# Softmax attention mixed with feature-map attention on one core: VectorE gets more key tiles in the first three query blocks, and the first score slots are computed in halves

## The chip, the cores and the metric

The kernel runs on one core of a Trainium2 chip. The metric is device time in microseconds (us) of one execution. Five engines work side by side, each through its own list in order: TensorE (PE in the profile, its weight loads PEld), ScalarE (ACT), VectorE (DVE), GpSimd (POOL) and SyncE (SP), which here issues most DMAs.

## The reference, cut to what matters

Two attentions of 32 heads with 16 channels each read the same x (2048 rows of 512). A replaces the exponential by a small learned feature map and is linear in the length; B is plain softmax attention. A gate of x mixes the two.

```python
q, k, v = (x @ wqkv) in heads                       # for A and for B, each with its own wqkv, wo
# A: phi = softmax(+-(q @ w_phi)); o = phi_q @ (phi_k^T v) / (phi_q @ sum(phi_k))
# B:
scores = einsum("bhqd,bhkd->bhqk", q, k) * Dh**-0.5
p = softmax(scores)
o = einsum("bhqk,bhkd->bhqd", p, v)
out = g * (o_A @ wo_A) + (1 - g) * (o_B @ wo_B)     # g = sigmoid(x . gate_w)
```

The bulk is B: 32 heads times 2048 by 2048 exponentials.

## The kernel before, in words

**Blocks, tiles, slots.** B is cut into 32 blocks. A block is a chunk of 512 queries for four heads (i = 0 to 3). For each of its heads there are 16 key tiles (kt = 0 to 15) of 128 keys, so a block has 64 score tiles of 128 keys by 512 queries. Blocks 0 and 1 use the same keys (row 0 of kT_B) and the same queries, with the two parities of qz.

**Two engines make exponentials.** Most tiles go to ScalarE, two tiles of one PSUM pair at a time: a *slot*. TensorE writes the two score tiles side by side (qk_mm, L990), ScalarE takes the exponential of 1024 columns in one instruction (add_exp, L1080) into one of the 12 slots of the buffer E (ERING, L76). The other tiles go to VectorE: it turns a score tile into int16 that, read as bf16, is a rough exponential (L1066; two tiles joined in one instruction of 1024 columns, L1056, where TABLE's "pairs" says so). Four such tiles are a group; GpSimd adds a constant to a group's words twice (shifted, L1042), and the three versions are each multiplied with V, so that a tile of VectorE costs three products with V and a tile of ScalarE one. DN (L31) says how many tiles of each block VectorE takes. Before, the VectorE tiles of a block are the last key tiles of each head (L912); next_tile gives ScalarE the others, counted up from 0 (L918).

**Closing a block.** All products with V of a block (L1101) add up in one PSUM bank, psO. When the last is done, VectorE copies psO to Tf (L1196), and only then can the products of the next block begin. Until then ScalarE can run ahead by the 12 slots of E.

**Start.** The first 512 rows of x come by two DMAs (L673, one issued by SP, one by ACT), are turned by TensorE against an identity (X0 to X3, L1494) and copied out (Xe0 to Xe3, L1500 on ACT for Xe1, L1503 on DVE for the others). The other three chunks of x come by DMA transposes, issued by SP one after the other (L678: x1_0 to x1_3, x2_0 to x2_3, x3_0 to x3_3). Keys and queries of chunk 0 come first: Q0.00 and Q0.01 are the two 256-column halves of the query product (L867, copied out by L874 on ACT and L876 on DVE), K0.00 makes key tile 0 (L824, copied out by L830 on ACT), K0.01 the key tiles 1 to 3 (copied out by L832 on DVE). K0.1, K0.2, K0.3 make the keys of the chunks 1 to 3 (L750 for the products, L817 for the copies). Before all that TensorE runs eight products of constants (warm, L701).

**Order.** Nothing is decided at run time. TABLE (L81) holds for each engine the full order of its operations as numbers, the place of each in the order of creation; place() walks these lists, and -1 in TensorE's list stands for an idle filler, four products with a zero weight (zero_mm, L1091). Before there are 14 fillers, all in the first blocks. Numbers of SP before: 0 is the first x DMA, 15 and 16 are weights for queries and values of the first heads, 2 to 13 are the DMA transposes x1_0 to x3_3, 17 to 19 the rest of the B weights, 20 to 27 DMA transposes of A's weights (wat).

Of the kernel before, what the change touches and what calls it, by code (L numbers as in the profile page):

```python
# [590 lines left out]
def _build(ctx, nc, A_x, A_wqkv, A_w_phi, A_wo, B_wqkv, B_wo, gate_w, out):  # L591
# [106 lines left out]
    def warm_fn(e):  # L698
        ins = None
        for _ in range(8):  # L700
            ins = e.matmul(psM, lhsT=ones[:, 0:128], rhs=ones, start=True, stop=True)  # L701
        return ins
# [927 lines left out]
```

## Time and profile before

| | us |
|---|---|
| median of 3 runs (662.16 to 662.63) | 662.53 |
| the profiled execution, own time | 662.22 |
| its span, first to last instruction | 660.4 |
| ACT busy in the span | 639.3 |
| DVE busy in the span | 603.7 |
| POOL busy in the span | 403.9 |

PE's busy time (651.3 us) is that of matmuls whose ends are modelled and overlap, so it is not to be read as the load of the array. The time of 662.22 us lies 1.8 us above the span: work around the first and the last instruction that the trace does not show.

### The profile page before, as it was taken

The page shows a single profiled execution, that of the slowest core. Times are in us where ns is not written, and L with a number is a line of the kernel's source. Part 1 is how long each engine was busy: PE and PEld are TensorE (multiplying, and loading weights), DVE is VectorE, ACT ScalarE, POOL GpSimd, SP SyncE. Part 2 cuts the span into 40 slices and gives each one's busy share as a digit, 9 for nine tenths or more (in the row PEclk, how much of TensorE's full clock was granted, in tenths as well). Part 3 has the DMA queues.
Part 4 walks back from the last instruction along what each step waited for, and adds up shares of the span by engine and source line. Part 5 has one row for each costly group of instructions (what it writes and reads, how often), then busy time and mean ns, then how long its engine had stood idle before and what let it go on. Part 6 is the DMA issues. An engine that isn't in the chain of part 4 may idle for free.

```text
span 660.4 us, 20511 instructions
## 1 busy us (share of the span) xinstructions
PE 651.3 (99%) x8752; PEld 228.4 (35%) x8752; DVE 603.7 (91%) x971; ACT 639.3 (97%) x723; POOL 403.9 (61%) x431
## 2 busy tenths in 40 slices
PE   9999999999999999999999999999999999999997
PEld 4332333434333333433333233322333233332333
DVE  4699889999998898999999999999999989999985
ACT  6999999999999999999999999999989999999996
POOL 7058457565665437575566776576766657665853
PEclk9999999999999999999999999999999999999999
DMA  6530101001010000000113221123201333024231
GB/s 136 106 91 11 34 7 28 11 7 31 6 28 11 12 18 10 16 20 11 25 40 92 78 41 53 47 65 76 59 26 60 94 82 72 18 67 108 58 80 36
DMA packets 67915, 30.94 MB, mean 47 GB/s; under 512 B 53176, under 2 KB 62776, under 8 KB 67824
## 3 DMA queue, kind: packets, MB, share of 16 engines
q1 hardware_dynamic: 66352, 28.95, 18.6%
q8 instruction: 69, 1.13, 0.7%
q10 hardware_dynamic: 1088, 0.66, 0.3%
q0 software_dynamic: 384, 0.02, 0.1%
q14 instruction: 22, 0.18, 0.1%
HBM read 7.87 MB, written 8.88 MB: 25 GB/s over the span
## 4 chain that ended last, share of the span: by engine, by line
PE 70%; ACT 22%; DVE 8%; issue 1%; POOL 0%; POOLq 0%
PE psO L1101 26%; PE psS L990 24%; ACT E_t L1080 20%; PE psS L750 13%; DVE Tx_t L1066 2%; PE psS L1382 2%; PE psS L841 1%; DVE oT_t L1066 1%; ACT EA_t L1375 1%; DVE Tz_t L1066 1%; DVE Ty_t L1066 1%; PE psS L1479 1%; PE psS L854 1%; ACT phiK_t L1375 1%; PE psS L701 1%
## 5 line engine op out<-in xcount | busy, mean ns | idle before, releaser
L1080 ACT ACTIVATE E_t<-psS 128x1024 bf16<-128x1024 f32 x652 | 610.6, 1095 | 9.5 <-PE psS L990 8.6
L990 PE MATMUL psS<-qz_t,kTB_t 32*128 32x512 bf16 x2048 | 271.0, 384 | 3.8 <-ACT E_t L1080 1.8
L1066 DVE TENSOR_SCALAR Tx_t<-psS 128x512 int16<-128x512 f32 x252 | 166.3, 681 | 8.8 <-PE psS L990 7.7
L990 PEld LDWEIGHTS psS<-qz_t,kTB_t 32*128 32x128 bf16 x2048 | 73.8, 91 | 229.3 <-ACT E_t L1080 109.4
L1101 PE MATMUL psO<-E_t,vaug_t 128*32 128x512 bf16 x1304 | 124.0, 385 | 0.5 <-DVE Tf_t L1196 0.3
L1066 DVE TENSOR_SCALAR Ty_t<-psS 128x512 int16<-128x512 f32 x122 | 81.1, 682 | 5.8 <-PE psS L990 4.8
L1042 POOL INT64_ADD vA_t<-vA_t x72 | 71.4, 995 | 15.1 <-PE psO L1101 13.7
L1042 POOL INT64_ADD Ty_t<-Ty_t x42 | 43.5, 1037 | 19.3 <-PE psO L1101 19.3
L1042 POOL INT64_ADD Ty_t<-Tx_t x29 | 30.0, 1036 | 37.1 <-DVE Tx_t L1066 33.0
L1101 PE MATMUL psO<-vA_t,vaug_t 128*32 128x512 bf16 (+1 forms) x520 | 50.5, 384 | 0.1
L1101 PEld LDWEIGHTS psO<-E_t,vaug_t 128*32 128x32 bf16 x1304 | 31.4, 95 | 43.8 <-issue 31.9
L1066 DVE TENSOR_SCALAR Tz_t<-psS 128x512 int16<-128x512 f32 x64 | 43.0, 683 | 1.9 <-PE psS L990 1.5
L1101 PE MATMUL psO<-Ty_t,vaug_t 128*32 128x512 bf16 (+1 forms) x436 | 44.2, 384 | 0.0
L1066 DVE TENSOR_SCALAR oT_t<-psS 128x512 int16<-128x512 f32 x60 | 40.3, 681 | 2.1 <-PE psS L990 1.7
L1042 POOL INT64_ADD vA_t<-Tx_t x22 | 22.6, 1029 | 29.4 <-DVE Tx_t L1066 21.5
L1066 DVE TENSOR_SCALAR WAT_t<-psS 128x512 int16<-128x512 f32 x58 | 38.9, 681 | 0.9 <-PE psS L990 0.5
L1066 DVE TENSOR_SCALAR vA_t<-psS 128x512 int16<-128x512 f32 x58 | 38.6, 682 | 0.7 <-PE psS L990 0.6
L1066 DVE TENSOR_SCALAR Wp_t<-psS 128x512 int16<-128x512 f32 x54 | 36.5, 683 | 1.4 <-PE psS L990 0.8
L1042 POOL INT64_ADD WoA_t<-Tz_t x18 | 19.5, 1082 | 27.5 <-DVE Tz_t L1066 27.4
L750 PE MATMUL psS<-xT_t,WB_t 128*32 128x512 bf16 x480 | 36.0, 383 | 0.1
L750 PE MATMUL psS<-Wp_t,xT_t 128*32 128x512 bf16 x512 | 35.8, 382 | 0.0
L1042 POOL INT64_ADD oT_t<-Ty_t x18 | 17.8, 991 | 20.4 <-DVE Ty_t L1066 19.0
(162 smaller groups left out, 873.2 us busy)
## 6 DMA issues: line engine op xcount, KB each, us to landing
dpq<-EA_t SPq DMA_DIRECT2D x16, 256.0 KB, 2.1
Rb_t<-lr SPq DMA_DIRECT2D x120, 32.0 KB, 1.9
dpo<-kv_t SPq DMA_DIRECT2D x16, 128.0 KB, 1.8
qz_t<-qz_t SPq DMA_DIRECT2D x120, 16.0 KB, 1.8
Tf_t<-Tf_t SPq DMA_DIRECT2D x60, 32.0 KB, 2.0
WB_t<-in_B_wqkv_dram SPq DMA_DIRECT2D x3, 384.0 KB, 3.7
out_dram<-WvA_t SPq DMA_DIRECT2D x8, 128.0 KB, 2.0
out_dram<-WB_t SPq DMA_DIRECT2D x6, 128.0 KB, 1.9
```

The source lines that it names most:

```text
L701: ins = e.matmul(psM, lhsT=ones[:, 0:128], rhs=ones, start=True, stop=True)
L750: ins = e.matmul(out[32 * i:32 * i + 32, :], lhsT=lhsT[:, 32 * i:32 * i + 32], rhs=rhs, start=start, stop=stop, tile_position=(0, 32 * i))
L841: mms = [lambda e, ap, i=i, t=t: e.matmul(ap[:, 128 * i:128 * (i + 1)], lhsT=xT[:, t, NQ * c + 128 * i:NQ * c + 128 * (i + 1)], rhs=W_B[:, ...
L854: mms = [lambda e, ap, i=i, t=t: e.matmul(ap[:, 256 * i:256 * (i + 1)], lhsT=xT[:, t, NQ * c + 128 * (2 * hf + i):NQ * c + 128 * (2 * hf + ...
L990: return e.matmul(bank, lhsT=kT_B[32 * i:32 * i + 32, ROW[b // 2] % 2, 128 * kt:128 * (kt + 1)], rhs=qz[32 * i:32 * i + 32, b // 2 % 4, b ...
L1042: op = P.add("pool", P64 + W64 * size, d_prio(g["ts"][0]) - 5.0 + (0.0 if key == "s" else M_LATE), lambda e: e.int64_add(words(dst), words ...
L1066: ops.append(drain(f, mm, "dve", 0.70, d_prio(d), lambda e, ap, q=q: e.tensor_scalar(quarter(tb, q).bitcast(I16), ap, EXPB, 0.0, op0=ALU.a ...
L1080: op = P.add("act", EXP_OVH + 0.4267 * n, 0.0, lambda e: e.activation(Ebuf[:, j // 2 % EPAIRS, 512 * SZ[0] * (j % 2):512 * SZ[0] * (j % 2) ...
L1101: return e.matmul(psO[32 * i:32 * i + w, :], lhsT=vaug[:, kt, o:o + w], rhs=rhs, start=start, stop=stop, tile_position=(0, 32 * i), skip_g ...
L1375: ins = e.activation(dst.rearrange("p (g s c) -> p s g c", s=2, c=64)[:, sgn, :, :], ap.rearrange("p (g c) -> p g c", c=64), ACTF.Exp, sca ...
L1382: mms = [lambda e, ap, n=n, f=f: e.matmul(ap[:, 64 * n:64 * n + 64].rearrange("p (s g j) -> p s g j", s=2, j=4), lhsT=ident[:], rhs=es[n][ ...
L1479: mms = [lambda e, ap, g=g: e.matmul(ap[:, 64 * g:64 * g + 64], lhsT=qT(g)[:, 128 * j:128 * (j + 1)], rhs=kzbd[:, g, 0:64], start=True, st ...
```

## The change

DN's first three entries go from 6, 20, 20 to 16, 24, 18: 58 instead of 46 VectorE tiles, and so 646 instead of 652 ScalarE slots. SOON names the key tiles that VectorE takes in the blocks 0 and 1: in block 0 the last of each x chunk (3, 7, 11, 15) for all four heads, in block 1 also 14 and 13. ScalarE gets the others in rising order. HALVES = 3: the first three slots are computed in two halves of 256 queries; the three first halves need only the first half of the queries. The first x chunk comes by four DMAs of 128 rows, each with its own landing; the value weights of the first heads move from SP to ACT. The key product of the first chunk is in three pieces (key tile 0, key tile 1, key tiles 2 and 3). The warm-up has six products, and the waits that tied V0.0 and the second query half to other work are gone.

```diff
-DN = (6, 20, 20, 24, 26, 26, 26, 20, 22, 22, 24, 18, 26, 24, 20, 26, 30, 22, 24, 26, 22, 24, 30, 26, 18, 22, 36, 18, 24, 24, 32, 16)
+DN = (16, 24, 18, 24, 26, 26, 26, 20, 22, 22, 24, 18, 26, 24, 20, 26, 30, 22, 24, 26, 22, 24, 30, 26, 18, 22, 36, 18, 24, 24, 32, 16)
...
+HALVES = 3
+SOON = ((3, 7, 11, 15), (3, 7, 11, 15, 14, 13))
...
-    for i in range(2):
-        dma(("sp", "act")[i], -0.01, lambda e, i=i: e.dma_start(
-            xs[:, 2 * i:2 * i + 2, :], A_x[0, 256 * i:256 * (i + 1), :].rearrange("(i p) c -> p i c", p=128)), [("xs", 2 * i), ("xs", 2 * i + 1)],
+    for i in range(4):
+        dma(("sp", "act")[i % 2], -0.01, lambda e, i=i: e.dma_start(xs[:, i, :], A_x[0, 128 * i:128 * (i + 1), :]), [("xs", i)],
...
-        for _ in range(8):
+        for _ in range(6):
...
-        for n, (lo, hi) in enumerate(((0, 128), (128, NQ))):
+        for n, (lo, hi) in enumerate(((0, 128), (128, 256), (256, NQ))):
...
-            if n == 0:
-                for op in q_half[1]:
-                    op.deps = op.deps + [ke]
...
-        for op in q_half[1]:
-            op.deps = op.deps + q_half[0]
...
-            dtiles.append(dict(t=(b, i, NT - dcount[b][i]), k=k))
+            dtiles.append(dict(t=(b, i, SOON[b][k // 4] if b < len(SOON) else NT - dcount[b][i]), k=k))
...
-                    t = (cur, i, done[cur][i])
+                    t = (cur, i, own[cur][i][done[cur][i]])
...
+        if j < HALVES:
+            for n in range(2):
+                def part(e, n=n):
+                    for m, t in enumerate(ts):
+                        ins = qk_mm(e, t, psS[:, 512 * (f.bank.index + m) + 256 * n:512 * (f.bank.index + m) + 256 * (n + 1)], n)
+                    return ins
...
+        if j < HALVES:
+            ops = []
+            for h in range(2):
+                def part(e, h=h):
+                    cols = slice(256 * h, 256 * (h + 1))
...
-    second = add_qk(1)
-    for op in P.ops:
-        if op.name == "V0.0.0":
-            op.deps = op.deps + [second]
+    add_qk(1)
```

TABLE is replaced as a whole: all five orders, "pairs" (38 joined VectorE instructions before, 56 after) and the PSUM banks. TensorE's list has 2 fillers instead of 14, GpSimd's 433 entries instead of 427, and VectorE's 966 instead of 971. In VectorE's list 62, 87 and 116 instructions stand ahead of the copies that close the blocks 0, 1 and 2 (59, 82 and 111 before); 6, 9 and 11 of them are joined ones (1, 1 and 3 before). The first line of SP's order:

```diff
-        0, 15, 16, 2, 3, 4, 5, 6, 7, 9, 8, 13, 10, 12, 11, 25, 23, 27, 24, 21, 17, 26, 20, 22, 128, 19, 18, 28, 129, 942, 943, 1066, 1068,
+        0, 17, 2, 4, 5, 6, 7, 9, 10, 11, 8, 12, 28, 15, 21, 13, 19, 14, 25, 24, 26, 22, 30, 29, 23, 132, 27, 133, 967, 968, 20, 1094,
```

In the new numbers 0 and 2 are the x DMAs of rows 0 to 127 and 256 to 383, 17 the first query weights, 4 to 15 the transposes x1_0 to x3_3, 28 a transpose of A's weights, 21 and 19 the rest of the value and query weights (384 KB each). So the last piece of the third chunk, 14 (x3_2), stands behind 28, 21 and 19. ACT issues 1 (x rows 128 to 255), 16 (key weights), 3 (x rows 384 to 511) and 18 (value weights), and then runs Xe1, the copy of K0.00, the copy of the first query half, and the halves of the slots 1, 2, 0, first halves first. TensorE's list begins warm, X0, X1, K0.00, Q0.00, K0.01, X2, X3, the first halves of the slots 1, 2 and 0, Q0.01, K0.02, their second halves, V0.0.

More of the change, by code (lines that the diff above doesn't have):

```diff
@@ L357 @@
-        "25040123"
+        "6706724520747524307462074350234503254104261046230540135230526350263502356105431043620541304205360462105410346013546026104264052301"
+        "2513052035065420642560520632560235102241054250613056452056240624506205462450264045260452405265402065246024502640532650642056236052"
+        "4504620523605642053265042604526406524062406524065260245560425650246054265042502654062554026054260542654306520456204254062540562403"
+        "0642560452065240526045625064265032065246024650420562305246024560235065240642360235602460254052410651360253065230645205320654256024"
@@ new lines @@
+        "6052605206520465424063260244502604241061254065204562406250462503260546206240562405264506205462504625406256034206524065246025064526"
+        "0624506426054260545260243061542146026045204526405625042654062540526045426045265024650426025604652402654062045625046256024605246054"
+        "2605624025054526052306246052452042560420534256406254016532054362045246504250624052356025604256032506325042045260456245026045624056"
+        "2045620524654065240562356023650245042560425063460253620320253230562540624602546054205426056240625406520356324305425065246052605320"
@@ new lines @@
+        "4354103461063510643013015042065240652460452064526045240625605260256045204520625046524650245604256406524065204526540620563250304640"
+        "5620542654206526024506425064250624603256024506254062540526406425046240563205632053602360230642650246506325032506245604265024502406"
+        "5236024546204650624604526402425406310360234504520635461502145054264062504625045216450620452640526045625406240625640254064250632502"
+        "4065230562406532045304526044205246054260426052450265406254026504256054260542062460542065240625406256045265042052545026506325062405"
@@ L358 @@
+        "642054205046206"
     ),
@@ L808, in _build @@
     kv_mm, va_free, wp_ops = [], [], []
-    kkey = lambda r, kt: ("kT", 0, "a") if r == 0 and kt < 1 else ("kT", r % 2, kt // 4)
+    kkey = lambda r, kt: ("kT", 0, "ab"[kt]) if r == 0 and kt < 2 else ("kT", r % 2, kt // 4)
     xk = lambda c: [("xT", t, c) for t in range(KT)]
@@ L817, in k_fill @@
         drain(f, mm, eng, 0.69, prio, lambda e, ap: e.tensor_copy(kT_B[:, r % 2, NQ * c:NQ * (c + 1)], ap),
-              writes=[("kT", r % 2, c)] + [("kT", 0, "a")] * (r == 2 and c == 0), name=f"Ke{r}.{c}")
+              writes=[("kT", r % 2, c)] + [("kT", 0, "a"), ("kT", 0, "b")] * (r == 2 and c == 0), name=f"Ke{r}.{c}")
     q_half = [[], []]
     def k_first(prio):
-        for n, (lo, hi) in enumerate(((0, 128), (128, NQ))):
-            f, mm = fill(prio + 0.15 * n - 0.015 * (n == 0), [lambda e, ap, t=t, lo=lo, hi=hi: e.matmul(
+        for n, (lo, hi) in enumerate(((0, 128), (128, 256), (256, NQ))):
+            f, mm = fill(prio + 0.15 * n, [lambda e, ap, t=t, lo=lo, hi=hi: e.matmul(
                 ap[:, lo:hi], lhsT=W_B[:, t, D:D + 128], rhs=xT[:, t, lo:hi], start=(t == 0), stop=(t == KT - 1))
-                for t in range(KT)], ["wbk0", ("xh", 0)] + [("xh", 1)] * n, EARLY, name=f"K0.0{n}", chunk=4, dur=0.08 if n == 0 else 0.2,
-                cols=hi - lo)
+                for t in range(KT)], ["wbk0", ("xi", 0), ("xi", 1)][:2 + (n == 1)] if n < 2 else ["wbk0", ("xh", 1)], EARLY, name=f"K0.0{n}", chunk=4,
+                dur=0.08 if n < 2 else 0.14, cols=hi - lo)
             kv_mm.append(mm)
@@ L832, in k_first @@
                 fn = lambda e, ap, lo=lo, hi=hi: e.tensor_copy(kT_B[:, 0, lo:hi], ap[:, lo:hi])
-            ke = drain(f, mm, "dve" if n else "act", 0.54 if n else 0.3, -20.5 if n else -21.0, fn, writes=[kkey(0, n)],
-                       name=f"Ke0.0{n}")
-            if n == 0:
-                for op in q_half[1]:
-                    op.deps = op.deps + [ke]
+            drain(f, mm, "dve" if n else "act", 0.54 if n else 0.3, -20.5 if n else -21.0, fn, writes=[kkey(0, n)],
+                  name=f"Ke0.0{n}")
     def v_fill(r, c, prio, banks=None):
@@ L917, in _build @@
     cur, rot = 0, 0
+    taken = {d["t"] for d in dtiles}
+    own = [[[kt for kt in range(NT) if (b, i, kt) not in taken] for i in range(4)] for b in range(NB)]
     def next_tile():
@@ L984, in _build, with qk_mm @@
     ramp_ops = list(P.readers[("S", 0)])
-    exp_ops, slot_fill = [None] * NS, {}
+    exp_ops, slot_fill, later = [None] * NS, {}, {}
     pv_last = []
-    def qk_mm(e, t, bank):
+    def qk_mm(e, t, bank, half=None):
         b, i, kt = t
+        cols = slice(0, NQ) if half is None else slice(256 * half, 256 * (half + 1))
         return e.matmul(bank, lhsT=kT_B[32 * i:32 * i + 32, ROW[b // 2] % 2, 128 * kt:128 * (kt + 1)],
-                        rhs=qz[32 * i:32 * i + 32, b // 2 % 4, b % 2, :], start=True, stop=True,
+                        rhs=qz[32 * i:32 * i + 32, b // 2 % 4, b % 2, cols], start=True, stop=True,
                         tile_position=(32 * i, 0))
@@ L1007, in fn @@
             return ins
+        if j < HALVES:
[4 more added lines that the diff above has]
+                    return ins
+                op = P.add("pe", 0.15, -100, part, reads=[k for k in reads if k[0] == "kT"], writes=[("S", j, n)],
+                           after=q_half[0][n:n + 1] + ([op] if n else []), name=f"qkh{j}.{n}")
+                op.kind, op.heads = "qk", [t[1] for t in ts]
+                P.readers.setdefault(("q", 0, 0), []).append(op)
+                if n == 0:
+                    op.acq, op.width = f, len(ts)
+            later[j] = op
+            return op
         op = P.add("pe", 0.25, -100, fn, reads=reads, writes=[("S", j)], name=f"qk{j}")
@@ L1079, in add_exp @@
         f = slot_fill[j]
+        if j < HALVES:
[3 more added lines that the diff above has]
+                    cols = slice(256 * h, 256 * (h + 1))
+                    o = 512 * SZ[0] * (j % 2)
+                    return e.activation(Ebuf[:, j // 2 % EPAIRS, o:o + 512 * n].rearrange("p (m c) -> p m c", c=NQ)[:, :, cols],
+                                        psS[:, 512 * f.bank.index:512 * (f.bank.index + n)].rearrange("p (m c) -> p m c", c=NQ)[:, :, cols],
+                                        ACTF.Exp, scale=ESCALE)
+                op = P.add("act", EXP_OVH + 0.2134 * n, 0.0, part, reads=[("S", j, h)], name=f"exph{j}.{h}")
+                op.kind = "exp"
+                ops.append(op)
+            op.rel = f
+            later[j].deps = later[j].deps + ops[:1]
+            P.join_writes(ops, ("E", j % ERING))
+            exp_ops[j] = op
+            return op
         op = P.add("act", EXP_OVH + 0.4267 * n, 0.0, lambda e: e.activation(
@@ L1509, in _build @@
         P.join_writes(xe[2 * n:2 * n + 2], ("xh", n))
+        P.join_writes(xe[n:n + 1], ("xi", n))
     for k in (("phiK", 0), ("phiK", 1)):
```

14 lines of the change are left out of this document (1 added, 13 removed), and 497 rows, old and new, of the table TABLE.

## Prediction

> **What bounds the kernel now.** The page comes first: its busy times, then its costliest groups.
>
> ```profile
> span 660.4 us, 20511 instructions
> PE 651.3 (99%) x8752; PEld 228.4 (35%) x8752; DVE 603.7 (91%) x971; ACT 639.3 (97%) x723; POOL 403.9 (61%) x431
> ...
> L1080 ACT ACTIVATE E_t<-psS 128x1024 bf16<-128x1024 f32 x652 | 610.6, 1095 | 9.5 <-PE psS L990 8.6
> ...
> L990 PEld LDWEIGHTS psS<-qz_t,kTB_t 32*128 32x128 bf16 x2048 | 73.8, 91 | 229.3 <-ACT E_t L1080 109.4
> ```
>
> PE and ACT both look full. The idle columns separate them. In 660 us ScalarE's exponentials stood still 9.5 us, while the weight loads of the score products sat idle 229.3 us, 109.4 us of it until an exponential freed a PSUM pair. PE waits for ACT far more than ACT for PE. Does that hold at the start too? ACT's timeline, the stretches up to the closing of blocks 0, 1, 2, and two late stretches:
>
> ```profile
> 5.21 0.60 ACT L1500 ACTIVATE xT_t<-psS 128x512 bf16<-128x512 bf16 x1 [2.13 <-PE psS L1494]
> 6.52 0.47 ACT L874 ACTIVATE qz_t<-psS,pmask_t 128x256 bf16<-128x256 f32 x1 [0.70 <-PE psS L867]
> 7.18 0.28 ACT L830 ACTIVATE kTB_t<-psS 128x128 bf16<-128x128 f32 x1 [0.19 <-PE psS L824]
> 8.01 21.43 ACT L1080 ACTIVATE E_t<-psS 128x1024 bf16<-128x1024 f32 x23 [0.56 <-PE psS L990]
> 29.69 23.28 ACT L1080 ACTIVATE E_t<-psS 128x1024 bf16<-128x1024 f32 x25 [0.25 <-PE psS L990]
> ```
>
> ```profile
> 8.00:42.60 34.60, 34.37 (x393) 13.15 (x393) 22.80 (x39) 34.19 (x37) 10.65 (x16) 1.00 0.54 119
> 8.00:56.80 48.80, 48.25 (x563) 17.81 (x563) 36.80 (x61) 48.39 (x53) 20.88 (x26) 1.00 0.39 86
> 8.00:77.40 69.40, 68.84 (x832) 23.89 (x836) 55.60 (x90) 68.99 (x76) 30.70 (x36) 1.00 0.31 69
> ```
>
> ```profile
> 76.40:150.00 73.60, 73.60 (x1042) 27.05 (x1035) 66.40 (x101) 72.91 (x87) 47.04 (x53) 1.00 0.07 14
> 150.00:650.00 500.00, 496.25 (x6738) 171.30 (x6738) 473.03 (x750) 491.70 (x556) 319.63 (x330) 1.00 0.19 47
> ```
>
> From 8.01 us on ACT runs exponentials back to back, with one gap of 0.25 us. VectorE (third busy column) has 34.6 - 22.8 = 11.8 us free until block 0 closes and 13.8 us until block 2 closes; afterwards it is free 7 us in 74 and 27 us in 500. So **ScalarE's count of slots sets the time**, and VectorE's free time lies in front.
>
> **The change part by part.**
>
> *Slots.* One costs 610.6 / 652 = 0.937 us. Six fewer: **-5.62 us**.
>
> *Halves.* Exponentials of 512 columns stand in two rows:
>
> ```profile
> L1375 ACT ACTIVATE EA_t<-psS 128x512 bf16<-128x512 f32 x32 | 19.3, 717 | 0.4 <-PE psS L750 0.4
> L1375 ACT ACTIVATE phiK_t<-psS 128x512 bf16<-128x512 f32 x32 | 18.6, 674 | 0.0
> ```
>
> They take 0.60 and 0.58 us of ACT, not half of 0.937 (0.47): a fixed part is paid twice. I take 0.59; six halves are 3.54 us, against 2.81 for three slots.
>
> *The first exponential.* What the chain up to 8.01 us is made of:
>
> ```profile
> DMA to landing us min/median/max: 3.3/3.5/3.7
> ...
> DMA to landing us min/median/max: 3.6/4.1/4.4
> ```
>
> ```profile
> 0.73 0.46 SPq L673 DMA_DIRECT2D phiK_t<-in_A_x_dram  x1
> 0.74 0.50 ACTq L673 DMA_DIRECT2D phiK_t<-in_A_x_dram  x1
> 1.27 0.50 ACTq L685 DMA_DIRECT2D WB_t<-in_B_wqkv_dram  x1
> ...
> 0.77 3.57 PE L701 MATMUL psS<-const-bfloat16-1.0 128*128 128x512 bf16 x8 [0.77 <-PEq L1615]
> ...
> 4.18 0.59 PE L1494 MATMUL psO<-ident_t,phiK_t 128*128 128x128 bf16 x4
> 4.56 1.06 PE L1494 MATMUL psS<-ident_t,phiK_t 128*128 128x128 bf16 x12
> ...
> 5.87 0.61 PE L867 MATMUL psS<-xT_t,WB_t 128*128 128x256 bf16 x4 [0.24 <-ACT xT_t L1500]
> ...
> 8.58 1.06 PE L841 MATMUL psS<-WB_t,xT_t 128*128 128x128 bf16 x16
> ```
>
> (The first landing row is that of x, the second that of the weights.) The warm-up ends 0.9 us sooner, but x does not: 0.73 + 3.3 gives 4.0 and 0.74 + 3.7 gives 4.4 us. Hence Xe1 at about 5.1 to 5.7. Key weights land at 1.27 + 4.1 = 5.4 us or so; K0.00's copy (0.28) follows Xe1, ending near 6.05, then the query's (0.47), ending near 6.85. A half score product and its latency (7.59 to 8.01 for a whole one) put the first half exponential at **7.3**. Three end at 9.07. The second halves need X2 and X3 on PE, and in VectorE's order K0.01's copy, a query copy, Xe2, Xe3 (0.4 to 0.5 each) and the second query half: about 9.5, after a hole of 0.4 us. Three more end at 11.27, where now three slots end at 8.01 + 2.81 = 10.82. **+0.45 us**, with ends at 0 (no hole) and +1.3 (the clock, below).
>
> *Chunk 3.* SP's rows:
>
> ```profile
> 2.30 16.10 SPq L678 DMA_TRANSPOSE xT_t<-in_A_x_dram  x12
> 18.44 6.71 SPq L688 DMA_TRANSPOSE WAT_t<-in_A_wqkv_dram  x5
> 25.19 0.58 SPq L685 DMA_DIRECT2D WB_t<-in_B_wqkv_dram  x1
> ...
> DMA to landing us min/median/max: 2.6/3.8/4.5
> ```
>
> A transpose occupies SP 1.34 us, a weight load 0.58. Now x3_2 stands behind twelve transposes and two loads: issued at 2.30 + 16.1 + 1.16 = 19.6, landed at 19.6 + 3.8 = 23.4 (last row: x). Products (1.05 us for 16) and copy (0.69) make the keys usable by about 25.4. ScalarE reaches its first chunk 3 tile in the 19th place of its order, 11.27 + 15 x 0.937 = 25.3. I take a wait of 0.3 us, between 0 and 2 (the loads share the DMA engines). Chunks 1 and 2 have 2 us to spare by the same count. **+0.3 us**.
>
> *VectorE and the closing of block 0.* Rows of VectorE:
>
> ```profile
> 18.95 0.69 DVE L817 CAST kTB_t<-psS 128x512 bf16<-128x512 f32 x1 [3.12 <-PE psS L750]
> 20.36 0.69 DVE L850 CAST vaug_t<-psS 128x512 bf16<-128x512 f32 x1 [0.72 <-PE psS L841]
> 21.62 0.69 DVE L1066 TENSOR_SCALAR Tx_t<-psS 128x512 int16<-128x512 f32 x1 [0.56 <-PE psS L990]
> 24.45 0.69 DVE L817 CAST kTB_t<-psS 128x512 bf16<-128x512 f32 x1 [2.14 <-PE psS L750]
> 25.73 1.23 DVE L1056 TENSOR_SCALAR Tx_t<-psS 128x1024 int16<-128x1024 f32 x1 [0.59 <-PE psS L990]
> 26.87 1.28 DVE L1066 TENSOR_SCALAR Tx_t<-psS 128x512 int16<-128x512 f32 x2
> ...
> 42.58 0.68 DVE L1196 COPY Tf_t<-psO 128x512 f32<-128x512 f32 x1
> ```
>
> Tiles follow each other in 0.60 us (1.28 for two, overlapping). Now VectorE waits for chunk 3 before nearly all of them; with key tiles 3, 7, 11 it can start near 10 us. Ahead of block 0's closing copy stand 3 more instructions and 5 more joined ones: 3 x 0.60 + 5 x 0.60 = 4.8, so 22.8 + 4.8 = 27.6 us of work from 8 us on, plus 3 to 5 us of waiting for x: closed at 39 to 41. ScalarE must stop when E's 12 slots are full, at the start of slot 24 + 12 = 36: 11.27 + 33 x 0.937 = 42.2. The copy and the first products of block 1 (0.68 and about 0.6) still fit. Cost 0, but the cover is 0 to 2 us, where now it is 46.4 (slot 41) - 42.6 = 3.8. Blocks 1 and 2 have more: 36.8 + 13 x 0.60 = 44.6, so about 56.6, against 60.9 for slot 56; 63.4, so about 75.4, against 82.4 for slot 79.
>
> *TensorE and GpSimd.* 12 tiles with two more products each with V are 6 rounds of four, and 12 single score products stand for 6 pairs. Rows of a round and of two:
>
> ```profile
> 10.42 0.40 PE L1101 MATMUL psO<-E_t,vaug_t 128*32 128x512 bf16 x4
> 10.65 0.61 PE L1091 MATMUL psO<-xT_t,zero_t 128*32 128x512 bf16 x8
> ```
>
> A further round costs 0.21 us: +1.3, and 0 to +1.3 for the scores; the 12 fillers that go are 12 x 0.21 = 2.5. Nothing remains on balance. GpSimd's six more additions fall into a stretch where it is busy 10.65 of 34.6 us. Later blocks have the same work in a new order; ACT's idle time there (0.7 + 8.3 us) may move 1.5 us either way, taken as 0.
>
> Sum: -5.62 + 0.45 + 0.3 = -4.9. The profiled execution took 662.22, so 657.3; the runs' median lies 0.31 above it. I say **657.5**.
>
> **The rivals.**
>
> *The clock at the start.* The first transposes follow each other in (0.59 - 0.31) / 3 = 0.09 us, the products of the same shape after 8.58 in 0.056: the array sped up near 5 us, though the clock column says 1.00. With 2.7 us of warm-up and then a pause until 4.0, the speed-up may come after 8 us. Then K0.00, K0.01, X2 and X3 (16 x 0.05) and both query products (8 x 0.11) grow by 1.7 us, 1.0 or so on ACT's path: 658.5. [...]
>
> *VectorE closes block 0 late.* Every microsecond past about 41 stops ScalarE as long. For it: VectorE is left with about 1 us free up to block 2. Against it: most tiles no longer hang on chunk 3. Price 1 to 3.5 us: about 659.5.
>
> *Slower: chunk 3.* Now the closing at 42.6 follows the copy of chunk 3's keys (24.45) by 18.1 us of saturated VectorE. If x3_2 lands so late that this copy slips beyond 25 and the work behind it keeps that length, slot 36 waits: a copy at 29 closes block 0 at 47, a stop of 6 us, and ScalarE waits 3 us for keys on top where E hides none of it. It decides from about 29: 657.5 + 6 = 664. Against it: VectorE's tiles of chunk 3 are now 4 of 16.
>
> *The saving does not arrive.* The new order of the later blocks gives the 5 us back in waits like the 8.6 us on L990: 662.5.
>
> **How the numbers follow.** Chances: forecast 0.58 (655 to 658.4), clock 0.08, closing late 0.15, saving lost 0.07, slower 0.12. The range leaves out the slower case, half of the lost saving and a little below: **655.0 to 662.0**. A measurement of this kernel tells 0.2% (1.3 us) from no change. Faster 0.81, same 0.07, slower 0.12.
>
> **What would show it.** Right: exponentials 643 of 1024 and 6 of 512 columns, the latter near 0.59 us of ACT; the first near 7.3 us; ACT without gaps above 0.5 us from 11 to 80 us; VectorE free 1 to 2 us instead of 13.8 up to block 2; the closing copy of block 0 at 39 to 41. Wrong: a gap of ACT near 25 (chunk 3) or 42 us (closing), transposes at 0.1 us each beyond 6 us, or ACT's later idle time grown by several us.

## The result and the profile after

The changed kernel takes 661.86 us (median of 20 runs, 659.41 to 666.75), the kernel before 661.97 us in 20 runs (661.77 to 662.67): a ratio of 1.0009, 95% interval 0.9995 to 1.0022. It is the same time. The forecast of 0.7% was wrong, though the number lies in the range.

What the medians hide is the spread: 0.9 us before, 7.3 us after. Each run comes with its mean granted TensorE clock, the share of full speed that the chip let TensorE run at. Sorted by it, the changed kernel's times fall apart:

| granted clock of the run | runs of 20 | mean us |
|---|---|---|
| 1.0 | 9 | 660.80 |
| 0.997 | 3 | 661.69 |
| 0.995 | 4 | 664.47 |
| 0.992 and 0.990 | 4 | 666.40 |

The 65 runs of the kernel before in the experiments below all have 0.999 or 1.0. So there are two results: at full clock the change gives 1.2 us, not 4.9; and in 11 of 20 runs it loses 1 to 6 us to the clock. The profiled execution is one at full clock (660.73 us). Its page:

```profile
span 658.8 us, 20497 instructions
PE 648.9 (98%) x8736; PEld 227.2 (34%) x8736; DVE 607.0 (92%) x966; ACT 634.8 (96%) x720; POOL 408.9 (62%) x437
...
L1113 ACT ACTIVATE E_t<-psS 128x1024 bf16<-128x1024 f32 x643 | 602.7, 1091 | 12.5 <-PE psS L992 11.6
```

The work left as forecast: 643 exponentials, 602.7 us for 610.6. But ScalarE now stands idle 12.5 us ahead of them instead of 9.5, nearly always until TensorE delivers scores (L992). Where? Its timeline (start, length, count, and in brackets the idle time before):

```profile
7.32 1.57 ACT L1102 ACTIVATE E_t<-psS 128x512 bf16<-128x512 f32 x3 [0.90 <-PE psS L992]
9.26 1.57 ACT L1102 ACTIVATE E_t<-psS 128x512 bf16<-128x512 f32 x3 [0.36 <-PE psS L992]
10.80 8.70 ACT L1113 ACTIVATE E_t<-psS 128x1024 bf16<-128x1024 f32 x9
20.24 3.85 ACT L1113 ACTIVATE E_t<-psS 128x1024 bf16<-128x1024 f32 x4 [0.74 <-PE psS L992]
24.64 1.02 ACT L1113 ACTIVATE E_t<-psS 128x1024 bf16<-128x1024 f32 x1 [0.56 <-PE psS L992]
28.00 23.41 ACT L1113 ACTIVATE E_t<-psS 128x1024 bf16<-128x1024 f32 x25 [2.34 <-PE psS L992]
51.90 25.09 ACT L1113 ACTIVATE E_t<-psS 128x1024 bf16<-128x1024 f32 x27 [0.49 <-PE psS L992]
```

Read against the same rows of before (first exponential at 8.01, one hole of 0.25 us up to 53 us), four holes of 0.36, 0.74, 0.56 and 2.34 us stand between 9 and 28 us. They are 4.0 us, and the largest ends at 28.00. The two stretches that split there, before first, then after (columns: busy PE, PEld, DVE, ACT, POOL, granted clock, DMA share, GB/s):

```profile
8.00:30.00 22.00, 21.90 (x275) 9.09 (x275) 10.20 (x18) 21.65 (x24) 6.34 (x11) 1.00 0.60 116
30.00:80.00 50.00, 49.53 (x602) 15.61 (x602) 47.09 (x77) 49.94 (x56) 26.22 (x26) 1.00 0.18 46
```

```profile
8.00:30.00 22.00, 19.50 (x241) 8.37 (x239) 18.70 (x29) 17.90 (x22) 11.24 (x17) 1.00 0.85 133
30.00:80.00 50.00, 49.51 (x618) 16.68 (x616) 45.46 (x69) 49.43 (x55) 26.91 (x28) 1.00 0.16 38
```

From 8 to 30 us ACT is busy 17.90 us instead of 21.65. The account of the two profiled executions: the first exponential comes 0.69 us earlier; the exponentials, halves included (602.7 + 3.1), take 4.8 us less than 610.6; the idle time between them grows from 8.9 to 12.9 us, by 4.0; the rest differs by 0.1. So -0.7 - 4.8 + 4.0 - 0.1 = -1.6, which is the difference of the spans (660.4 and 658.8).

What released the exponential at 28.00? TensorE's timeline around it, and SP's:

```profile
24.15 0.39 PE L992 MATMUL psS<-qz_t,kTB_t 32*128 32x512 bf16 x4
26.59 1.05 PE L754 MATMUL psS<-xT_t,WB_t 128*32 128x512 bf16 x16 [2.05 <-DMA xT_t<-in_A_x_dram]
```

```profile
13.90 2.28 SPq L692 DMA_TRANSPOSE WAT_t<-in_A_wqkv_dram  x1
...
17.54 0.58 SPq L689 DMA_DIRECT2D WB_t<-in_B_wqkv_dram  x1
...
19.40 0.57 SPq L689 DMA_DIRECT2D WB_t<-in_B_wqkv_dram  x1
20.02 1.19 SPq L682 DMA_TRANSPOSE xT_t<-in_A_x_dram  x1
```

K0.3, the key product of the third chunk, stands at a fixed place of TensorE's list. TensorE reaches it at 24.54, waits 2.05 us for x3_2, and everything behind it waits too, score products of earlier chunks among it. The exponential at 28.00 begins before VectorE has copied the new keys:

```profile
27.69 0.69 DVE L821 CAST kTB_t<-psS 128x512 bf16<-128x512 f32 x1 [2.12 <-PE psS L754]
...
37.96 0.68 DVE L1229 COPY Tf_t<-psO 128x512 f32<-128x512 f32 x1
```

The copy ends at 28.38. So ScalarE did not lack the keys of the third chunk; it lacked any score product, because TensorE's list stood still. The chain of waits has the DMA as its longest piece here:

```profile
20.02 6.33 DMA xT_t<-in_A_x_dram
```

SP issued x3_2 at 20.02, and it landed at 26.35, 6.33 us later. Both 384 KB weight loads were issued ahead of it, the second one 0.6 us ahead.

### The profile page after: what moved, and what is told of

It is laid out like the page before. It is cut to its first block, busy times and chain, and to the rows that moved or that the text cites. A ratio compares the mean times of both kernels' runs of the same rounds, so it can differ in the third digit from the quotient of the medians.

```text
span 658.8 us, 20497 instructions
## 1 busy us (share of the span) xinstructions
PE 648.9 (98%) x8736; PEld 227.2 (34%) x8736; DVE 607.0 (92%) x966; ACT 634.8 (96%) x720; POOL 408.9 (62%) x437
## 3 DMA queue, kind: packets, MB, share of 16 engines
q1 hardware_dynamic: 65840, 28.82, 19.8%
## 4 chain that ended last, share of the span: by engine, by line
PE 74%; ACT 14%; DVE 7%; SPq 3%; DMA 1%; issue 1%; DVEq 0%
PE psO L1134 28%; PE psS L992 26%; PE psS L754 14%; ACT E_t L1113 13%; PE psS L1415 2%; SPq L682 2%; DVE Tx_t L1082 2%; DVE oT_t L1082 1%; DMA xT_t<-in_A_x_dram 1%; DVE Ty_t L1082 1%; ACT EA_t L1408 1%; PE psS L855 1%; PE psS L842 1%; PE psS L1512 1%; PE psS L1455 1%
## 5 line engine op out<-in xcount | busy, mean ns | idle before, releaser
L1113 ACT ACTIVATE E_t<-psS 128x1024 bf16<-128x1024 f32 x643 | 602.7, 1091 | 12.5 <-PE psS L992 11.6
L992 PE MATMUL psS<-qz_t,kTB_t 32*128 32x512 bf16 (+1 forms) x2054 | 270.2, 383 | 3.0 <-DVE qz_t L877 0.4
L1082 DVE TENSOR_SCALAR Tx_t<-psS 128x512 int16<-128x512 f32 x252 | 167.1, 683 | 10.2 <-PE psS L992 8.5
L992 PEld LDWEIGHTS psS<-qz_t,kTB_t 32*128 32x128 bf16 x2054 | 72.7, 91 | 227.7 <-ACT E_t L1113 101.7
L1134 PE MATMUL psO<-E_t,vaug_t 128*32 128x512 bf16 x1292 | 120.7, 384 | 0.0
L1082 DVE TENSOR_SCALAR Ty_t<-psS 128x512 int16<-128x512 f32 x114 | 76.2, 681 | 3.9 <-PE psS L992 3.4
L1134 PE MATMUL psO<-vA_t,vaug_t 128*32 128x512 bf16 x520 | 52.8, 386 | 0.0
L1134 PE MATMUL psO<-Ty_t,vaug_t 128*32 128x512 bf16 x440 | 45.6, 384 | 0.0
L1082 DVE TENSOR_SCALAR WAT_t<-psS 128x512 int16<-128x512 f32 x52 | 35.4, 684 | 1.8 <-PE psS L992 1.5
L1082 DVE TENSOR_SCALAR vA_t<-psS 128x512 int16<-128x512 f32 x54 | 36.0, 683 | 0.9 <-PE psS L992 0.9
L1082 DVE TENSOR_SCALAR Wp_t<-psS 128x512 int16<-128x512 f32 x50 | 33.8, 681 | 1.3 <-PE psS L992 1.0
L1058 POOL INT64_ADD oT_t<-Ty_t x19 | 18.1, 953 | 26.2 <-DVE Ty_t L1082 25.5
L1134 PE MATMUL psO<-Tx_t,vaug_t 128*32 128x512 bf16 x288 | 29.4, 384 | 0.0
```

Of the source, the lines that this page charges most:

```text
L992: return e.matmul(bank, lhsT=kT_B[32 * i:32 * i + 32, ROW[b // 2] % 2, 128 * kt:128 * (kt + 1)], rhs=qz[32 * i:32 * i + 32, b // 2 % 4, b ...
L1058: op = P.add("pool", P64 + W64 * size, d_prio(g["ts"][0]) - 5.0 + (0.0 if key == "s" else M_LATE), lambda e: e.int64_add(words(dst), words ...
L1082: ops.append(drain(f, mm, "dve", 0.70, d_prio(d), lambda e, ap, q=q: e.tensor_scalar(quarter(tb, q).bitcast(I16), ap, EXPB, 0.0, op0=ALU.a ...
L1113: op = P.add("act", EXP_OVH + 0.4267 * n, 0.0, lambda e: e.activation(Ebuf[:, j // 2 % EPAIRS, 512 * SZ[0] * (j % 2):512 * SZ[0] * (j % 2) ...
L1134: return e.matmul(psO[32 * i:32 * i + w, :], lhsT=vaug[:, kt, o:o + w], rhs=rhs, start=start, stop=stop, tile_position=(0, 32 * i), skip_g ...
```

## Experiments

The theory after this: SP's order, with x3_2 behind three other transfers, costs both, the 2 us pause and, through it, the lowered clock. Two rivals: the pause matters because of the new tile choice, so that the same delay would cost the kernel before little; and the clock is a thing apart, due to the shorter warm-up or to the 12 fillers that went. The expectations say theory K for the cost of the late keys as such (in e8, that they cost only because of the new tile choice) and theory C for the cost of an array at half rate (0.50 for 3.4 us in e5's profile, from 401.2 to 404.6 us, and for 10.2 us, three times that, in e8's and e12's). The runs of the ten timed kernels in one table; "before" is the kernel before in the same comparison (30, 18 and 17 runs, all with a clock of 0.999 or 1.0).

| kernel | median us (runs) | before | ratio, 95% | runs with clock 0.999 up / 0.997 / lower | mean us at 0.999 up |
|---|---|---|---|---|---|
| after | 661.86 (20) | 661.97 | 1.0009, 0.9995 to 1.0022 | 9 / 3 / 8 | 660.80 |
| e1_x3_first | 659.45 (7) | 662.42 | 0.9965, 0.9953 to 0.9977 | 4 / 3 / 0 | 659.06 |
| e2_warm8 | 660.79 (11) | 662.42 | 0.9984, 0.9974 to 0.9994 | 7 / 3 / 1 | 660.41 |
| e3_fill_k3 | 662.87 (11) | 662.42 | 1.0008, 1.0000 to 1.0017 | 10 / 1 / 0 | 662.67 |
| e4_before_no_fillers | 667.33 (12) | 662.42 | 1.0057, 1.0028 to 1.0086 | 4 / 1 / 7 | 661.89 |
| e5_x3_warm8 | 660.13 (5) | 662.64 | 0.9962, 0.9950 to 0.9973 | 3 / 2 / 0 | 659.61 |
| e6_k2_early | 660.77 (6) | 662.64 | 0.9971, 0.9960 to 0.9982 | 5 / 1 / 0 | 660.57 |
| e7_before_warm6 | 663.90 (11) | 662.64 | 1.0015, 1.0006 to 1.0024 | 10 / 1 / 0 | 663.45 |
| e8_before_x3_late | 668.09 (6) | 662.64 | 1.0081, 1.0064 to 1.0097 | 0 / 2 / 4 | none |
| e9_x3_later | 663.62 (12) | 662.12 | 1.0021, 1.0003 to 1.0039 | 4 / 1 / 7 | 660.68 |
| e10_x3_fill398 | 660.01 (5) | 662.12 | 0.9969, 0.9957 to 0.9981 | 5 / 0 / 0 | 660.18 |

### The third chunk first in SP's order (e1_x3_first)

```diff
-8, 12, 28, 15, 21, 13, 19, 14, 25, 24,
+8, 12, 15, 13, 14, 28, 21, 19, 25, 24,
```

> The changed kernel with one edit: in SP's order the three transposes of x chunk 3 that stood behind a transpose of A's weights and two 384 KB weight loads are issued first (12, 15, 13, 14, then 28, 21, 19). In the changed kernel's profile x3_2 was issued at 20.0 us, landed at 26.3 us, and ScalarE stood still 2.3 us before 28.0 us. Theory K (the keys of chunk 3 come late and that hole eats the saving): x3_2 lands near 20 us, the 2.3 us hole is gone, 2 to 3 us faster than the changed kernel, so about 658 us in executions at full clock. Theory C (the array falls to half rate for one or more windows of 3.4 us; the spread of 659.4 to 666.8 us comes from that) splits: if the pause of TensorE before the chunk 3 keys starts it, the spread goes too and the granted clock is 1.00 in all runs, median 658; if it starts elsewhere (warm-up), runs with a clock of 0.990 to 0.997 remain and the median stays 2 us or more above the fastest.

It is the one edit that turns the change into a gain: 659.45 us, ratio 0.9965, and no run below a clock of 0.997. x3_2 is issued at 17.14 and lands 2.6 us later, at about 19.7. ScalarE's timeline:

```profile
24.59 1.02 ACT L1103 ACTIVATE E_t<-psS 128x1024 bf16<-128x1024 f32 x1 [0.56 <-PE psS L982]
25.82 23.40 ACT L1103 ACTIVATE E_t<-psS 128x1024 bf16<-128x1024 f32 x25 [0.21 <-PE psS L982]
```

TensorE reaches K0.3 at 24.41 and does not wait:

```profile
24.41 1.05 PE L744 MATMUL psS<-xT_t,WB_t 128*32 128x512 bf16 x16
```

The hole of 2.34 us is 0.21, and the profile's span is shorter by 2.1 us (656.7). The holes of 0.74 and 0.56 us ahead of it stay, so they are not of this transfer. The pause is a matter of SP's order, and with it go the deep falls of the clock: of the four kernels with chunk 3 first (e1, e5, e6, e10) 0 of 23 runs are below 0.997, of the three with x3_2 behind the loads and nothing in the pause (the changed kernel, e2, e9) 16 of 43. The expectation had 658 us and a clock of 1.00 in every run; 3 of 7 runs stay at 0.997, so something else still lowers the clock a little. e5 below shows one place.

### Two warm-up products more (e2_warm8)

```diff
-        for _ in range(6):
+        for _ in range(8):
```

> The changed kernel with eight warm-up products instead of six, nothing else. If theory C's half rate comes from the short warm-up, all runs have a granted clock of 1.00 and lie within 0.5 us of each other, near 660 to 661 us. If it comes from pauses later on, the spread of 659 to 667 us with clocks down to 0.99 stays. Theory K alone expects no difference but the start: 0 to 0.4 us later.

A small gain, 0.9984. The start does not move (first exponential at 7.39 us), but in its profile x3_2 was issued at 19.42 instead of 20.02, because the transpose of A's weights ahead of it occupied SP for 1.69 us instead of 2.28; TensorE's pause is 0.99 instead of 2.05, and the hole ahead of chunk 3 is 1.27 instead of 2.34. One of 11 runs has a clock below 0.997, against 8 of 20. That is neither of the two outcomes expected, and it decides nothing on the warm-up: whether the other runs had a short pause too is not known. e1, with six products and no run below 0.997, shows that a warm-up of six alone does not lower the clock that far.

### Fillers in the pause (e3_fill_k3)

```diff
-841, 874, 944, 117, 118,
+841, 874, 944, -1, -1, -1, -1, -1, -1, -1, -1, -1, -1, 117, 118,
```

> The changed kernel with ten fillers (zero products, 0.21 us each, 2.1 us) put into TensorE's list just ahead of the product for the chunk 3 keys, where TensorE waits 2.05 us for x3_2. They change no transfer: by theory K the hole of ScalarE stays at about 2.3 us and the time of full-clock runs at 659.5 to 661. Theory C with the pause as its start: the spread is gone, granted clock 1.00 in every run, median about 660.5. Theory C with another start: the spread stays.

Ten fillers of 0.2 us stand where TensorE would wait. First TensorE, then ScalarE, then the stretch 24 to 28 us:

```profile
24.38 2.34 PE L988 MATMUL psO<-xT_t,zero_t 128*32 128x512 bf16 x40
26.55 1.04 PE L618 MATMUL psS<-xT_t,WB_t 128*32 128x512 bf16 x16
```

```profile
27.95 23.40 ACT L977 ACTIVATE E_t<-psS 128x1024 bf16<-128x1024 f32 x25 [2.37 <-PE psS L856]
```

```profile
24.00:28.00 4.00, 4.00 (x69) 1.71 (x66) 1.84 (x4) 1.08 (x2) 1.04 (x1) 1.00 0.73 105
```

K0.3 still comes at 26.55 and ScalarE still waits 2.37 us: the fillers bring no data sooner. But PE is busy 4.00 of 4.00 us where the changed kernel has 1.95, and the clock stays up: none of 11 runs is below 0.997, against 8 of 20. So at this place it is TensorE's pause that lowers the clock. The median gains nothing, since at full clock this kernel runs as long as the one before (662.67 against 662.42), where the changed kernel is 1.2 us ahead of its own (660.80 against 661.97). In its profile 0.85 us of that difference of 1.4 is a hole at 648.45, near the end; why is open.

### The kernel before without its fillers (e4_before_no_fillers)

```diff
-802, 877, 803, -1, -1, 879, 224,
+802, 877, 803, 879, 224,
...
```

> The kernel before with its 14 fillers taken out of TensorE's list, warm-up of eight kept. Theory C, if fillers in the first blocks are what keeps the clock: the runs spread by 2 to 5 us, with granted clocks below 1.00. If the fillers do nothing: 661.5 to 662.7 us as before, clock 1.00 in every run.

All 14 fillers go. At full clock it is a little sooner than before (661.89 against 662.42), but 7 of 12 runs go down to 0.984 to 0.990, and the median is 667.33. Between 8 and 30 us PE is busy 19.41 us here, as in the changed kernel (19.50), against 21.90 before:

```profile
8.00:30.00 22.00, 19.41 (x231) 8.25 (x229) 10.44 (x17) 21.68 (x24) 6.38 (x11) 1.00 0.59 116
```

Fillers that I had counted as 2.5 us of work that goes away are what keeps the clock of the kernel before. The profiled execution is one at full clock, so where the clock falls in the others is not shown.

### The kernel before with its third chunk late (e8_before_x3_late)

```diff
-8, 13, 10, 12, 11, 25, 23,
+8, 10, 26, 13, 19, 11, 17, 12, 25, 23,
```

> The kernel before with the change's SP order for chunk 3: a transpose of A's weights and two 384 KB loads between its four transposes. Theory K says the lateness costs only because the change made ScalarE reach chunk 3 at its 19th slot (25 us) instead of the 25th (30.4 us): here ScalarE loses under 0.5 us near 25 to 30 us, though VectorE, which waits for chunk 3, starts 2 us later; time 661.5 to 663. If late keys cost the kernel before as much, 664 us, the hole is not owed to the new choice of tiles.

(26, a transpose of A's weights, and the loads 19 and 17 leave their later places in the list.) This gives the kernel before the SP order that the changed one has around its third chunk, and nothing else. The rival of the tile choice falls: with the old choice the loss is not small but 0.81% (5.45 us), more than either outcome expected. First TensorE, then ScalarE, then the stretches:

```profile
25.69 1.90 PE L740 MATMUL psS<-xT_t,WB_t 128*32 128x512 bf16 x16 [2.67 <-DMA xT_t<-in_A_x_dram]
```

```profile
28.16 1.02 ACT L1070 ACTIVATE E_t<-psS 128x1024 bf16<-128x1024 f32 x1 [2.84 <-PE psS L980]
...
31.19 1.02 ACT L1070 ACTIVATE E_t<-psS 128x1024 bf16<-128x1024 f32 x1 [2.00 <-PE psS L980]
```

```profile
22.00:24.60 2.60, 1.01 (x10) 0.25 (x8) 0.00 (x0) 2.60 (x4) 0.00 (x0) 1.00 1.48 137
24.60:28.00 3.40, 2.31 (x18) 0.63 (x18) 0.37 (x1) 0.72 (x1) 0.00 (x0) 0.51 0.70 135
28.00:31.50 3.50, 3.50 (x27) 0.61 (x25) 2.12 (x3) 1.34 (x2) 0.00 (x0) 0.50 0.49 111
31.50:34.80 3.30, 3.30 (x30) 1.04 (x23) 1.90 (x4) 2.29 (x3) 1.03 (x1) 0.50 0.00 0
34.80:38.00 3.20, 3.20 (x42) 1.35 (x43) 2.54 (x6) 2.53 (x4) 0.00 (x0) 0.99 0.00 0
```

TensorE is idle from 23.02 and waits 2.67 us for x3_2; the granted clock falls inside this wait and is 0.50 from 24.6 to 34.8 us, ACT's busy share falls to 1.34 of 3.50, and K0.3's 16 products take 1.90 instead of 1.05 us. One late transfer is paid twice, once as a wait and once as a half-speed array behind it. All six runs have a clock of 0.997 or less.

### Two more executions of the changed kernel (e11_after_look, e12_after_look)

Nothing is edited; the question is what a run at a lowered clock looks like.

> The changed kernel once more, for a profile of an execution with a lowered clock (11 of its 20 runs had one). Theory C with the pause as its start: if the granted clock is below 1.00, the clock record by stretches shows half rate in one to four windows of 3.4 us right behind TensorE's wait for x3_2 (24 to 27 us), and the products there have twice the step. If half rate lies at the start (before 10 us) or in the middle of the kernel instead, the pause is not what sets it off.

> A second look at the changed kernel, for the same reason and with the same expectations as the first.

The first took 659.66 us at clock 1.0, the second 664.83 at 0.992: the spread of the 20 runs, with a profile of each side. The second one's stretches and TensorE's row show the same as e8:

```profile
21.00:24.00 3.00, 2.87 (x37) 1.28 (x34) 3.00 (x5) 3.00 (x4) 1.13 (x2) 1.00 1.07 204
24.00:28.00 4.00, 2.25 (x27) 0.84 (x24) 1.74 (x3) 1.28 (x2) 1.04 (x1) 0.77 1.31 106
28.00:31.00 3.00, 3.00 (x20) 0.56 (x16) 1.98 (x3) 1.57 (x2) 1.21 (x2) 0.50 0.75 211
31.00:34.50 3.50, 3.50 (x26) 1.80 (x24) 1.98 (x3) 2.52 (x3) 0.84 (x1) 0.50 0.34 67
34.50:38.00 3.50, 3.50 (x37) 0.75 (x34) 2.53 (x5) 2.30 (x3) 0.45 (x1) 0.73 0.00 0
```

```profile
26.46 1.90 PE L754 MATMUL psS<-xT_t,WB_t 128*32 128x512 bf16 x16 [1.75 <-DMA xT_t<-in_A_x_dram]
```

The pause before K0.3 is 1.75 us, shorter than the 2.05 of the profiled execution at full clock, and yet the array runs at half speed behind it. The clock falls inside the pause, about 1.4 us after TensorE became idle at 24.71:

```profile
25.80:26.10 0.30, 0.00 (x0) 0.00 (x0) 0.00 (x0) 0.04 (x1) 0.27 (x1) 1.00 1.18 264
26.10:26.40 0.30, 0.00 (x0) 0.00 (x0) 0.00 (x0) 0.00 (x0) 0.30 (x1) 0.53 1.24 231
```

Counted from the rows, half of the clock is lost for 4.00 x 0.23 x 2 + 6.5 + 3.50 x 0.27 x 2 = 10.2 us. ScalarE's holes there are 3.10, 0.49, 0.49, 1.33 and 0.30 us, 5.7 instead of 2.34, and the run is 4.0 us above the full-clock mean. Six profiles have x3_2 behind the loads and no fillers in the pause. Their pauses are 0.19 (e9), 0.99 (e2), 1.34 (e11), 1.75 (e12), 2.05 (the changed kernel) and 2.67 us (e8), and the clock fell in those of 1.75 and 2.67. So whether a pause of about 2 us lowers the clock changes from run to run, and so does the length of the pause.

### The third chunk later still (e9_x3_later)

```diff
-19, 14, 25, 24,
+19, 25, 14, 24,
```

> The suspected wait doubled: the changed kernel with one more transpose of A's weights (25) ahead of x3_2, which then is issued 1.3 us later. Theory K: ScalarE's hole before 28 us grows from 2.3 to about 3.5 us, executions at full clock near 662. [...]

Meant to double the wait, it did not: x3_2 is issued at 20.60 and lands 5.3 us later at 25.87, sooner than in the changed kernel's profile. It therefore says nothing on the size of the wait. 8 of 12 runs are below 0.999, as with the changed kernel (11 of 20). In its profile the array reaches full speed late: the eight transposes X2 and X3 take 1.06 us from 6.76 on, against 0.61 in the changed kernel, and the halves begin at 8.19 us:

```profile
8.19 1.57 ACT L1092 ACTIVATE E_t<-psS 128x512 bf16<-128x512 f32 x3 [1.14 <-PE psS L982]
...
26.11 1.05 PE L744 MATMUL psS<-xT_t,WB_t 128*32 128x512 bf16 x16 [0.19 <-DMA xT_t<-in_A_x_dram]
```

The three slots end at 12.18 instead of 10.80, TensorE comes to K0.3 1.4 us later, and so it waits only 0.19 us for x3_2. The granted clock shows 1.00 all through this slow start, so a late start does not show in the sorting by clock.

### Can it be made better still? (e5_x3_warm8, e6_k2_early, e10_x3_fill398, e7_before_warm6)

Three kernels build on e1, and one tries the warm-up on the kernel before. e5 is e1 with `range(8)`:

> Both repairs in the changed kernel: chunk 3's transposes first, and eight warm-up products. Measured so far at full clock: the changed kernel 660.8 us, with chunk 3 first 658.7, with eight warm-ups 660.4. If the late transpose (theory K) and the half-rate windows (theory C) are the two causes and they are separate, this gives 658.3 to 659.0 us in every run, clock 1.00, median 3 to 4 us under the kernel before. If pauses of TensorE after the start also set off half-rate windows, some runs with 0.997 or less remain, up to 661.7.

It gives 0.9962, the same as e1, with 2 of 5 runs at 0.997; the 658.3 to 659.0 us hoped for did not come. In its profile the first half exponential comes at 7.91 us instead of 7.26: the eight warm-up products run until 4.34, and the first transposes begin at 4.14 instead of 3.54. (In e2's profile the array was at full speed by then, 0.39 us for four transposes against 0.63, and it came at 7.39.) One half-speed stretch, 401.2 to 404.6 us, costs about 1 us, far from any start:

```profile
398.00:401.20 3.20, 3.05 (x50) 1.48 (x46) 3.20 (x7) 3.20 (x5) 1.46 (x2) 1.00 0.03 5
401.20:404.60 3.40, 3.40 (x32) 1.14 (x30) 2.66 (x5) 2.40 (x3) 1.46 (x2) 0.50 0.00 0
```

No pause like that of K0.3 stands ahead of it: PE is busy 3.05 of 3.20 us, but 24 of its 50 products there (L1489) have only 4 columns. e1's profile has them too and stays at full clock. Whether they set the stretch off is not shown. e10 is e1 with one filler on either side of that place:

```diff
-3475, 563, 3398,
+3475, -1, 563, 3398,
...
-566, 3480, 3401,
+566, 3480, -1, 3401,
```

> The changed kernel with chunk 3 first, plus two fillers (0.43 us of TensorE) near 398 us, around the small Z products of the feature-map half, where the profiles of the two kernels with eight warm-ups and chunk 3 first show one half-rate window (401.2 to 404.6 and 401.6 to 405.1 us). If the thin stretch of TensorE there sets that window off, no run has 0.997 any more (chunk 3 first alone: 3 of 7) and all lie at 658.4 to 659.5 us. If not, runs with 0.997 and 660 to 662 us remain. Should the fillers be in the way of real work, the time at full clock rises by up to 0.4 us.

All five runs are at 1.0, where e1 has 3 of 7 at 0.997; so few runs do not show that the fillers did it. Their mean is 660.18, above the 659.06 of e1's runs at full clock, so nothing is gained. In its profile 0.45 us of that is a hole at 400.41, beside the fillers; others stand at 546 us, far from them. e6 is e5 with the key product of the second chunk earlier, against the hole of 0.74 us:

```diff
-924, 830, 869, 927, 107, 108, 109, 110,
+924, 107, 108, 109, 110, 830, 869, 927,
```

(VectorE's copy, 111, moves from the fifth place behind 106 to the third, and some PSUM banks in TABLE change with it.)

> The kernel of the run before this one, with the keys of chunk 2 earlier: TensorE runs K0.2 two score slots ahead of its place, VectorE frees its bank with D1 of tile 7 head 1 ahead of a joined pair and copies the keys two places sooner. In the changed kernel's profile ScalarE stood still 0.74 us at 20.2 us, just behind that copy (18.97 to 19.66). If the order of the keys (theory K, wider: every x chunk is now needed on the tick) makes that hole, it goes, and the time falls by 0.5 to 0.8 us. If something else holds the slot (its PSUM pair), nothing changes.

```profile
19.69 1.02 ACT L923 ACTIVATE E_t<-psS 128x1024 bf16<-128x1024 f32 x1 [0.52 <-PE psS L802]
...
21.20 4.20 ACT L923 ACTIVATE E_t<-psS 128x1024 bf16<-128x1024 f32 x4 [0.48 <-PE psS L802]
```

The hole of 0.74 becomes two of 0.52 and 0.48; 660.77 is no gain over e5, where 0.5 to 0.8 us had been expected. The first of the two ends on score products that now stand behind K0.2 (TensorE runs them at 19.01). So moving the product in TensorE's list moves the hole; it does not close it. e7 gives the kernel before a warm-up of six:

> The kernel before with six warm-up products instead of eight; its 14 fillers stay. Theory C with the warm-up as a start of half-rate windows: some runs with a granted clock of 0.997 or less, 2 us or more above the others. If only the fillers matter: 661.5 to 662.7 us, clock 1.00 in all runs.

663.90 us, ratio 1.0015, with 10 of 11 runs at 0.999 or more: so the short warm-up alone does not lower the clock as in the changed kernel. Why its runs at full clock take 663.45 us, 0.8 more than the kernel before, is open.

**A version that beats both kernels** is e1: the change with x3_2 ahead of the weights, 659.45 against 662.42 us, 0.35% (0.23 to 0.47%). The three built on it are as fast within their intervals.

## Why the prediction was wrong, step by step

- **Slots**: right. 643 + 3 pairs of halves; 1024-column exponentials at 602.7 / 643 = 0.937 us each.
- **Halves**: right in kind, a little too dear. The group of the six in the changed kernel:

```profile
L1102 ACT ACTIVATE E_t<-psS 128x512 bf16<-128x512 f32 x6 | 3.1, 598 | 1.3 <-PE psS L992 1.3
```

  They took 3.1 us, 0.52 each; I took 0.59 from the exponentials of the feature maps. The hole between them was 0.36 (taken 0.4).
- **The first exponential**: right in the number, 7.32 for 7.3, in part by luck. The copies of K0.00 and of the first query half end sooner than forecast (5.78 for 6.05, 6.42 for 6.85), and the score product then waits 0.42 us for VectorE's query copy, which I had not counted. The three slots end at 10.80 for 11.27, 0.5 us better.
- **Chunk 3**: the step that failed. "I take a wait of 0.3 us, between 0 and 2." The issue at 19.6 was nearly right (20.02). The landing, "19.6 + 3.8 = 23.4", was 26.35: I took the median of the transposes for one that goes out behind two large loads, though I wrote that "the loads share the DMA engines" (loads and transposes of SP are in one queue of the page, q1, with 19.8% of the 16 engines). TensorE reaches K0.3 at 24.54, so 23.4 would have cost nothing and 26.35 costs 2.05, and ScalarE 2.34. I had also looked at the wrong reader. I counted when ScalarE needs its first chunk 3 tile; what decided was the place of K0.3 in TensorE's list, which holds up all products behind it. Shown by e1 (the wait goes) and by e8 (the old kernel gets it).
- **"Chunks 1 and 2 have 2 us to spare"**: the transfers had, the slots had not. The holes of 0.74 and 0.56 us are there in e1 too. The last piece of the second chunk was issued at 11.28 and landed at 14.6, but K0.2 has its place in TensorE's list where it begins at 17.87, and VectorE's copy of these keys ends at 19.66, when ScalarE had been idle since 19.50. The second hole ends on score products that stand behind a value product (L842):

```profile
17.87 1.05 PE L754 MATMUL psS<-xT_t,WB_t 128*32 128x512 bf16 x16
...
18.97 0.69 DVE L821 CAST kTB_t<-psS 128x512 bf16<-128x512 f32 x1
...
23.15 1.07 PE L842 MATMUL psS<-WB_t,xT_t 128*128 128x128 bf16 x16
```

  From 8 to 24 us TensorE is busy 15.55 of 16.00 us, so it has little room to run either product sooner. This is read from the rows; apart from e6 no run varied it.
- **VectorE and the closing of block 0**: right in its cost, 0, and too cautious in its sizes. Block 0 closed at 37.96, forecast 39 to 41; block 1 at 56.88 for 56.6, block 2 at 77.27 for 75.4. VectorE kept 7 us free up to block 2, not the 1 to 2 forecast:

```profile
8.00:77.20 69.20, 66.21 (x813) 23.93 (x811) 62.22 (x94) 64.53 (x72) 38.15 (x44) 1.00 0.39 69
```

- **TensorE and GpSimd, "nothing remains on balance"**: true of the profiled execution's busy times, but the fillers' going was counted only as work saved. What they covered, the clock, was not named. e4 shows their worth in the kernel before: 4.9 us of the median.
- **The sum**: 657.3 was forecast for the profiled execution and 660.73 came, 3.4 more: chunk 3 +2.0, the two holes ahead of it +1.3, the start -0.5, and some 0.5 less of ACT's time filled from 30 to 80 us. The median (661.86) lies another 1.1 us above the profiled execution, where I had allowed 0.2; that is the runs with a lowered clock.
- **The rivals.** *The clock at the start* had the right actor and, for most of the price, the wrong place. In the changed kernel's profile the array was at full speed in time; in e9's, which starts with the same operations, it was late, and the slots ended 1.4 us later, near the 1.0 of this rival. That the speed-up would come after 8 us was my estimate, and its 1.7 us takes each product at twice its step, where the start of the kernel before shows 0.09 for 0.056 us; twice was seen at a clock of 0.50, with 1.90 for the 1.05 us of K0.3 (e8, e12). What cost more came in K0.3's pause, where I had not linked a late transfer with the clock: the runs at 0.995 and less take 4 to 6 us more, not 1. *Chunk 3* as the slower case was right in "ScalarE waits 3 us" and wrong in the rest: the copy at 27.69 did not close block 0 late, since 4 of VectorE's 16 tiles hang on it, and the 18.1 us of work did not keep their length. *The saving does not arrive* came near in its number (662.5 for 661.86) by a way that it did not name, which is luck.

## What to carry to other kernels

In lists that run in order, a transfer is due when its first reader's *engine* comes to it, not when the bound engine needs the result: look up that place before a DMA is put behind others. Leave a margin for its landing behind large loads: here the median on record (3.8 us) and even the longest (4.5) would both have shown no wait, and 6.33 came. A pause of 2 us on TensorE cost 2.1 us of the span at full clock (658.8 against 656.7 with chunk 3 first), and the runs with the lowest clock take 5.6 us more again (666.40 against 660.80); work that seems to do nothing may be what keeps the array up (without its 14 fillers 7 of 12 runs of the kernel before are at 0.990 or less, with them none of 65 below 0.999). Where half the runs differ by 4 us, sort the runs by granted clock before reading any one profile, and look at the start apart, since e9's slow start showed a clock of 1.00.
